# Clustered attention and a gated MLP on one core: key tiles of exp with their own users, no constant matmuls, a new order

## The chip, the cores and the metric

One Trainium2 chip, one core. The metric is the device time of one execution in microseconds (us). The kernel before took 648.9 us, the median of three runs (647.11 to 650.06).

## The reference

Masked attention over 4 batches, 8 heads, 768 positions of 64 values, then an MLP with a spatial gate for each batch. All in fp32.

```
q_assign = argmax(q/|q| @ centroids/|c|, -1); k_assign = argmax(k/|k| @ centroids/|c|, -1)   # 16 clusters
scores = where(q_assign[:, None] == k_assign[None, :], q @ k.T / 8, -1e9)
attn = softmax(scores); x = attn @ v                        # per head; heads side by side: x is 768 x 512
h = relu(x @ w_in); u, v = h[:, :512], h[:, 512:]           # w_in 512 x 1024
v_n = (v - mean(v)) / sqrt(var(v) + 1e-6)
out = (u * (w_spatial @ v_n + b_spatial[:, None])) @ w_out  # w_spatial 768 x 768, w_out 512 x 512
```

## The kernel before

**Numbers in two halves.** Every fp32 factor that needs its precision is split in an fp16 high half and an fp16 low half, and one product is the sum of the products of the halves. So each group of matmuls has a `hi` and a `lo` part.

**The work.** There are 16 head pairs, n = 0 to 15, four of them per batch. A pair goes through `prep` (load, split, cluster logits on PE, argmax on DVE), `shifts` (per head: plain scores on PE at L1029 and their maxima on DVE at L1036, each maximum 128x512; then two 0/1 flag columns and a shift column written by ACT at L1055 and L1058, turned by DMA and put back as extra rows of the factors) and `attend` (L1167). In `attend`, for each head and two key tiles at a time: three score groups of two matmuls (L1204, L1206), three exps on ACT (L1211) that write fp32 into a tile `p32`, for each of the two key tiles a CAST on ACT to the fp16 high half (L1226) and a subtraction on POOL for the low half (L1227), and 18 value matmuls on PE (L1233). The heads of pairs 9, 11, 13 and 15 go through `turned` (L1082) instead, with the queries on the partitions: scores L1104 and L1106, maxima on DVE L1114, a scale column `sl` and a bias column `bi` on DVE (L1127, L1128 per tile; L1130, L1131 two tiles at once in pair 15), exp L1140, cast L1150, POOL L1151, a DMA transpose L1152, and value matmuls L1159 to L1161. After each four pairs `mlp(b)` (L1294) runs the MLP of that batch: 324 matmuls of 512 columns at L1305, in groups of 6: tiles of v, tiles of u, the spatial product, and the output tiles, with ACT, DVE and POOL between them.

**Buffers.** PSUM results come from one ring `r_acc` with 8 banks, each given to whoever is next. The fp32 results of exp come from a ring of two tiles `p32`, each holding a pair of key tiles:

```
r_p32 = R(wk, "p32", [P, 2, S], F32, P32_BUFS)          # P32_BUFS = 2
```

In this ring the tile of two pairs ago must be released by all its users, so by the POOL subtractions of both key tiles, before the first exp of the new pair may be written.

**What sets the order.** The kernel writes no instruction directly. Each `op` names its engine, its cost and what it waits for; the class `Plan` (L310) then runs a small model of the core and puts one operation after another into the program, at each step on the engine that could start first the ready one with the smallest due time. The due times are a table of numbers, `STARTS`, one per operation in the order in which the operations are declared. The model adds two pads: `LATE_PAD` to the end of DMAs of the later stages, and `PE_PAD` to the lag of anything that PE waits for. So an operation is put where the model says that its inputs are there, a little later than it would be without pads. What the chip then does is wait for semaphores in the order written.

**Constant matmuls.** `keep_warm` (L658) declares matmuls of a tile of ones with itself (L662), 512 columns, whose result nobody reads. Their key is so high that the plan takes one only where PE has nothing else ready at that moment. There are 145 of them from the list `WARM` (model times from 2.0 us on) and 5 (`WARM_END`) ahead of the last output tile. All of the 145 write one PSUM token, so one bank of the eight is held from the first of them to the last:

```
tok, o = r_acc.new(), None
...
    o = op("PE", 0.2145, run, after=after, at=at, use=[tok] if k else [], new=[] if k else [tok], cols=512, key=FILLER + k, mms=1)
```

## Time and profile before

| | us |
|---|---|
| median of three runs | 648.9 |
| the runs | 647.11, 650.06, 648.9 |
| profiled execution, its own time | 649.11 |
| span of that execution | 647.3 |
| PE busy | 631.8 (98%) |
| ACT busy | 466.3 (72%) |
| POOL busy | 442.2 (68%) |
| DVE busy | 419.6 (65%) |
| DMA engines, share of the span (queues q1, q10, q8, q14) | 61.0%, 3.0%, 0.6%, 0.1% |
| chain that ended last | PE 68%, ACT 5%, DVE 3%, DMA 2%, issue 1%, POOL 1% |

The time of an execution is its span and 1.8 us around it. Busy time of PE counts the whole run of a matmul; since matmuls overlap in the array, a row that says 0.38 us for one of 512 columns does not mean that the next one starts 0.38 us later. The granted clock (`PEclk`) is a share of full speed.

### The profile page before, as it was taken

The page shows a single profiled execution, that of the slowest core. Times are in us where ns is not written, and L with a number is a line of the kernel's source. Part 1 is how long each engine was busy: PE and PEld are TensorE (multiplying, and loading weights), DVE is VectorE, ACT ScalarE, POOL GpSimd, SP SyncE. Part 2 cuts the span into 40 slices and gives each one's busy share as a digit, 9 for nine tenths or more (in the row PEclk, how much of TensorE's full clock was granted, in tenths as well). Part 3 has the DMA queues.
Part 4 walks back from the last instruction along what each step waited for, and adds up shares of the span by engine and source line. Part 5 has one row for each costly group of instructions (what it writes and reads, how often), then busy time and mean ns, then how long its engine had stood idle before and what let it go on. Part 6 is the DMA issues. An engine that isn't in the chain of part 4 may idle for free.

```text
span 647.3 us, 16908 instructions
## 1 busy us (share of the span) xinstructions
PE 631.8 (98%) x6753; PEld 381.7 (59%) x6753; DVE 419.6 (65%) x845; ACT 466.3 (72%) x879; POOL 442.2 (68%) x376
## 2 busy tenths in 40 slices
PE   8999999999999999999999999999999999999997
PEld 3577767776666765546555755565556555444443
DVE  5989799898999977665776796477523860231000
ACT  5789889899999995536887997689778864232121
POOL 3577888878999995337777885698789964253020
PEclk9999999999999999999999999999999999999999
DMA  6676977697557767622778897976883579212233
GB/s 191 151 126 153 158 172 180 141 174 172 135 123 177 164 139 143 144 60 66 166 157 157 176 217 135 169 156 137 144 155 74 101 142 199 58 34 65 55 76 98
DMA packets 175173, 88.01 MB, mean 136 GB/s; under 512 B 159315, under 2 KB 162422, under 8 KB 175094
## 3 DMA queue, kind: packets, MB, share of 16 engines
q1 hardware_dynamic: 171350, 80.24, 61.0%
q10 hardware_dynamic: 3744, 6.69, 3.0%
q8 instruction: 53, 0.87, 0.6%
q14 instruction: 26, 0.21, 0.1%
HBM read 27.66 MB, written 6.29 MB: 52 GB/s over the span
## 4 chain that ended last, share of the span: by engine, by line
PE 68%; ACT 5%; DVE 3%; DMA 2%; issue 1%; POOL 1%; POOLq 0%; ACTq 0%
PE acc L1305 37%; PE acc L1233 9%; PE acc L1204 5%; PE acc L1206 5%; PE acc L1029 4%; ACT p L1140 2%; PE acc L1104 2%; PE acc L1106 2%; DMA pt<-pt 2%; PE acc L662 1%; DVE nm L1114 1%; PE acc L1159 1%; PE acc L1160 1%; PE acc L1161 1%; DVE lo L912 1%
## 5 line engine op out<-in xcount | busy, mean ns | idle before, releaser
L1227 POOL TENSOR_TENSOR pt<-p,pt 128x768 f16<-128x768 f32 x136 | 226.8, 1687 | 36.2 <-ACT pt L1226 26.8
L1036 DVE TENSOR_REDUCE nm<-acc 128x1 f32<-128x512 f32 (+1 forms) x216 | 137.4, 680 | 25.3 <-PE acc L1029 23.1
L1211 ACT ACTIVATE p<-acc 128x512 f32<-128x512 f32 x216 | 118.7, 607 | 22.4 <-PE acc L1206 12.5
L1305 PE MATMUL acc<-win,xT 128*128 128x512 f16 x576 | 134.1, 379 | 0.1
L1226 ACT CAST pt<-p 128x768 f16<-128x768 f32 x136 | 111.1, 845 | 10.6 <-PE acc L1233 3.5
L1305 PE MATMUL acc<-vn,wsp 128*128 128x512 f16 x432 | 100.7, 379 | 0.0
L1233 PEld LDWEIGHTS <-pt 128*128 128x128 f16 x2448 | 87.8, 97 | 15.8 <-issue 0.7
L1151 POOL TENSOR_TENSOR pt<-p,pt 128x768 f16<-128x768 f32 x48 | 79.3, 1664 | 25.8 <-ACT pt L1150 21.7
L1233 PE MATMUL acc<-vhl,pt 128*128 128x65 f16 x2448 | 93.2, 193 | 0.3 <-POOL pt L1227 0.3
L1305 PEld LDWEIGHTS <-xT 128*128 128x128 f16 x576 | 54.8, 98 | 61.5 <-issue 0.5
L1204 PE MATMUL acc<-hq,lo 128*128 128x512 f16 (+1 forms) x288 | 82.0, 325 | 1.5 <-ACT p L1211 1.3
L1206 PE MATMUL acc<-hq 81*128 81x512 f16 (+1 forms) x288 | 82.2, 326 | 0.3 <-DMA hq<-sht 0.3
L1029 PE MATMUL acc<-hq 80*128 80x512 f16 (+1 forms) x288 | 71.4, 325 | 2.6 <-ACT p L1211 2.4
L1377 POOL TENSOR_TENSOR ghl<-u,ghl 128x512 f16<-128x512 f32 x24 | 27.8, 1157 | 64.8 <-ACT ghl L1376 63.6
L1305 PE MATMUL acc<-wou,gT 128*128 128x512 f16 x288 | 67.7, 379 | 1.1 <-ACT o L1395 0.6
L1305 PEld LDWEIGHTS <-wsp 128*128 128x128 f16 x432 | 40.9, 97 | 46.0 <-issue 0.2
L1140 ACT ACTIVATE p<-acc,bi,sl 128x512 f32<-128x512 f32 (+1 forms) x96 | 57.1, 680 | 12.1 <-POOL pt L1151 7.3
L1375 DVE SCALAR_TENSOR_TENSOR u<-acc,bsp,u 128x512 f32<-128x512 f32 x24 | 17.9, 748 | 69.8 <-PE acc L1305 69.7
L1114 DVE TENSOR_REDUCE nm<-acc 128x1 f32<-128x512 f32 (+1 forms) x72 | 46.3, 682 | 11.1 <-PE acc L1106 11.0
L1305 PEld LDWEIGHTS <-gT 128*128 128x128 f16 x288 | 27.6, 98 | 32.9 <-DMA gT<-ghl 1.1
L662 PE MATMUL acc<-ones 128*128 128x512 f16 x150 | 44.3, 397 | 1.6 <-DVE ones L621 1.6
L1150 ACT CAST pt<-p 128x768 f16<-128x768 f32 x48 | 39.3, 842 | 7.3 <-DMA pt<-pt 5.9
(156 smaller groups left out, 1055.6 us busy)
## 6 DMA issues: line engine op xcount, KB each, us to landing
raw<-in_kqT_dram SPq DMA_DIRECT2D x15, 768.0 KB
vraw<-in_vp_dram SPq DMA_DIRECT2D x16, 384.0 KB
out_dram<-o ACTq DMA_DIRECT2D x24, 256.0 KB
hq<-hq SPq DMA_DIRECT2D x15, 384.0 KB
vn<-in_w_in_dram SPq DMA_DIRECT2D x8, 512.0 KB
hq<-lo SPq DMA_DIRECT2D x15, 192.0 KB
lo<-hq SPq DMA_DIRECT2D x15, 192.0 KB
wraw<-in_wsT_dram SPq DMA_DIRECT2D x12, 192.0 KB
```

Source lines behind the costliest of these rows:

```text
L1029: T.matmul(out=acc.t[:, c:c + cs.stop - cs.start], lhsT=hq.t[0:R_SH, 1, h, t * P:(t + 1) * P], rhs=hq.t[0:R_SH, 0, h, cs], start=c == 0, s ...
L1036: V.tensor_reduce(out=nm.t[:, t, k:k + 1] if n == 1 else nm.t[:, t:t + n, k], in_=src, axis=AX.X, op=ALU.max, negate=True)
L1114: V.tensor_reduce(out=nm.t[:, t, k:k + 1] if n_ == 1 else nm.t[:, t:t + n_, k], in_=src, axis=AX.X, op=ALU.max, negate=True)
L1140: A.activation(out=p32.t[:, j, halves[x]], in_=sc.t[:, j * (S - 512):(j + 1) * (S - 512)] if x else sc.t, func=AF.Exp, bias=bi.t[:, t:t + ...
L1151: c = op("POOL", 1.64, lambda pt=pt, j=j, p32=p32: G_.tensor_tensor(out=pt.t[:, S:], in0=p32.t[:, j, :], in1=pt.t[:, 0:S], op=ALU.subtract ...
L1204: T.matmul(out=o, lhsT=lo.t[:, h, ks], rhs=hq.t[:, 2, h, cs], start=x == 0, stop=False, skip_group_check=True)
L1206: T.matmul(out=o, lhsT=hq.t[0:R_E, 0, h, ks], rhs=hq.t[0:R_E, 1, h, cs], start=False, stop=True, skip_group_check=True)
L1211: o = op("ACT", 0.6, lambda: A.activation(out=p32.t[:, j0:j0 + n_, cs], in_=sc.t.rearrange("p (t c) -> p t c", t=n_), func=AF.Exp, bias=P_ ...
L1226: o = op("DVE" if fast else "ACT", C_CAST if fast else 0.83, lambda pt=pt, p32t=p32t, fast=fast: (V.tensor_copy if fast else A.copy)(out=p ...
L1227: o = op("POOL", 1.64, lambda pt=pt, p32t=p32t: G_.tensor_tensor(out=pt.t[:, S:], in0=p32t(), in1=pt.t[:, 0:S], op=ALU.subtract), after=[o ...
L1233: T.matmul(out=a[:, c * W:c * W + w], lhsT=lhsT, rhs=rhs, skip_group_check=True, **f)
L1305: T.matmul(out=acc.t[:, 0:w], lhsT=lr[m][0], rhs=lr[m][1], start=(m == 0), stop=(m == n - 1))
```

## The change

- `p32` is one constant tile of four key tiles, with two rings of two: in each pair of key tiles each one has a ring of its own, and is released by its own cast, subtraction and value matmuls. The memory is the same as before, 4 x 768 fp32 values on each partition.
- The 150 constant matmuls are gone (`WARM` and `WARM_END` empty), and with them the PSUM bank that they held.
- The two flag columns of a head are written by one ACT instruction (128x6x2) instead of two of 128x6; 25 fewer in all. The low half of the value sums (`wl`) is written in fp16 by DVE directly, which drops 12 ACT instructions at L804. `bsp` is scaled on POOL instead of DVE, once. In pair 15 `sl` and `bi` are computed per tile, as in pairs 9, 11 and 13: 12 + 12 DVE instructions of one column instead of 6 + 6 of two.
- Both pads are zero, and `STARTS` is a new table. The options `FLAG_POOL` and `SHC_POOL` are empty.

The diff, cut (`STARTS` is shown by a part of its first row):

```diff
-MEAN_LOG = 11
...
-LATE_PAD = 0.4
+LATE_PAD = 0.0
+EARLY_PAD = 0.0
...
-PE_PAD = 0.1
+PE_PAD = 0.0
...
 STARTS = (
-    "c-rmR)0Uu3kcHuNWJcuI)vR_`wOMW3wr$(CZQHhO+qP|U{<AroE131(#Ix5H3|L&2pVeSV*d<n*t!2;IDAt<AWARx83ug...
+    "c-jruV}l+#5J2H1lbP^cwcGA)ZQHhO+qP}nwr$(CZQH*0Kb+^oiO%9N#UfY&7RuVNIIK2X%6hR(44GuWh-v1TWrjJ%STK...
...
-WARM = (2.0, 2.3, 2.6, ...
-WARM_END = 5
+WARM = ()
+WARM_END = 0
...
-TS1 = (9, 11, 13)
+FLAG_POOL = ()
+SHC_POOL = ()
...
-            early = not o.tag or o.tag.startswith("p1") or o.tag[0] in "pcvwmf" and o.tag[1] == "0"
-            o.dma, o.post = o.dma * part, o.post + (0.0 if early else LATE_PAD)
+            o.dma, o.post = o.dma * part, o.post + (LATE_PAD if o.tag else EARLY_PAD)
...
-    r_p32 = R(wk, "p32", [P, 2, S], F32, P32_BUFS)
+    p32s = const.tile([P, 4, S], F32, name="p32")
+    r_p32 = [R(None, "p32%d" % j, None, None, 2, tiles=[p32s[:, 2 * (i ^ j) + j] for i in range(2)]) for j in range(2)]
...
-        o = op("DVE", 0.07, lambda: V.tensor_scalar(out=bsp, in0=bsp, ...
+        o = op("POOL", 0.22, lambda: G_.tensor_scalar(out=bsp, in0=bsp, ...
...
-        l_ = op("DVE", 0.3, lambda: V.scalar_tensor_tensor(out=w32.t[:, :, 0:m], in0=svr(), ...
-        l_ = op("ACT", 0.28, lambda: A.activation(out=wl.t[:, :, 0:m], in_=w32.t[:, :, 0:m], func=AF.Copy, scale=2.0 ** MEAN_LOG), ...
+        l_ = op("DVE", 0.28, lambda: V.scalar_tensor_tensor(out=wl.t[:, :, 0:m], in0=svr(), ...
...
-                for c in range(2):
-                    u = 2.0 ** (-MEAN_LOG * c)
-                    cols.append(op("ACT", 0.22, lambda ...: A.activation(out=sx.t[:, t0:t1, R_E + c], ..., bias=-u, scale=2 * u / LIM), ...))
+                def flags(nl=nl, sx=sx, t0=t0, t1=t1):
+                    src = nl.t[:, t0:t1].unsqueeze(2).broadcast_to([P, t1 - t0, 2])
...
+                        A.activation(out=sx.t[:, t0:t1, R_E:R_END], in_=src, func=AF.Relu, bias=-1.0, scale=2.0 / LIM)
+                cols.append(op(*(("POOL", 0.25) if n in FLAG_POOL else ("ACT", 0.23)), flags, after=[o, c_sh, m_half], use=[nl, sx], key=KS))
...
-            p32 = r_p32.new()
+            p32 = [r.new() for r in r_p32]
...
-            if n in TS1:
-                ys = []
-                for t in range(t0, t0 + 2):
...
-            else:
-                o = op("DVE", 0.14, lambda z=z: V.tensor_scalar(out=sl.t[:, z], in0=nl.t[:, z], ...
-                o = op("DVE", 0.15, lambda z=z: V.scalar_tensor_tensor(out=bi.t[:, z], in0=nl.t[:, z], ...
-                ys = [o, o]
+            ys = []
+            for t in range(t0, t0 + 2):
...
-                c = op("ACT", 0.83, lambda ...: A.copy(out=pt.t[:, 0:S], in_=p32.t[:, j, :]), after=got, use=[p32], new=[pt], key=K_HI)
+                c = op("ACT", 0.83, lambda ...: A.copy(out=pt.t[:, 0:S], in_=p32[j].t), after=got, use=p32[j:j + 1], new=[pt], key=K_HI)
```

The change in `attend` is the same in kind as the last lines: each user names `p32[k % 2]` where it named `p32`, and the exp that spans two key tiles writes a slice of `p32s`.

**How the order moves.** On PE at the start, before, around the first maxima of the second head pair: `hq` are the factors, `acc` PSUM banks, `ones` the constant tile.

```order
L662 LDWEIGHTS ones_76
L662 MATMUL acc0_112<-ones_76 128x512
L1029 LDWEIGHTS hq_177
L1029 MATMUL acc2_114<-hq_177 128x256
L1029 LDWEIGHTS hq_177
L1029 MATMUL acc2_114<-hq_177 128x256
L662 LDWEIGHTS ones_76
L662 MATMUL acc0_112<-ones_76 128x512
L1029 LDWEIGHTS hq_177
L1029 MATMUL acc6_118<-hq_177 128x512
```

The same place after the change:

```order
L1026 LDWEIGHTS hq_171
L1026 MATMUL acc6_119<-hq_171 128x512
L1026 LDWEIGHTS hq_171
L1026 MATMUL acc0_113<-hq_171 128x256
L1026 LDWEIGHTS hq_171
L1026 MATMUL acc0_113<-hq_171 128x256
L1026 LDWEIGHTS hq_171
L1026 MATMUL acc4_117<-hq_171 128x512
L925 LDWEIGHTS hq_269
L925 MATMUL acc1_114<-cmw_96,hq_269 128x2x16
```

The constant matmuls between the L1029 matmuls (L1026 after the change) are gone, the bank `acc0` that they wrote holds scores, and the cluster logits of the next pair (L928, now L925) stand right behind.

On PE in the middle of the program, before, where the value matmuls of a key tile (`pt`) end and the first MLP matmuls of a later tile (`win`, `xT`) begin:

```order
L1233 MATMUL acc2_114<-vhl0_84,pt2_107 128x65
L1233 LDWEIGHTS pt2_107
L1233 MATMUL acc2_114<-vhl0_84,pt2_107 128x64
L1233 LDWEIGHTS pt2_107
L1233 MATMUL acc2_114<-vhl0_84,pt2_107 128x65
L662 LDWEIGHTS ones_76
L662 MATMUL acc0_112<-ones_76 128x512
L1305 LDWEIGHTS xT1_100
L1305 MATMUL acc6_118<-win_98,xT1_100 128x512
L1305 LDWEIGHTS xT1_100
```

After the change, in the middle as well, at the end of a spatial group (`wsp`, `vn`):

```order
L1301 LDWEIGHTS wsp_101
L1301 MATMUL acc0_113<-vn_103,wsp_101 128x512
L1301 LDWEIGHTS wsp_101
L1301 MATMUL acc0_113<-vn_103,wsp_101 128x512
L1301 LDWEIGHTS wsp_101
L1301 MATMUL acc0_113<-vn_103,wsp_101 128x512
L1106 LDWEIGHTS hq_3251
L1106 MATMUL acc5_118<-lo_3290,hq_3251 128x512
L1108 LDWEIGHTS hq_3251
L1108 MATMUL acc5_118<-hq_3251 128x512
```

Before, a constant matmul stands between value matmuls and MLP matmuls; after, score matmuls follow the MLP matmuls at once, and `acc0` holds a spatial product.

On ACT, before, where the flag columns (`shx`) are written from the maxima (`nl`) of a head, among the exps of another:

```order
L1211 ACTIVATE p32_776<-acc2_114 128x512
L1055 ACTIVATE shx0_81<-nl_773 128x6
L1058 ACTIVATE shx0_81<-nl_773 128x6 x2
L1211 ACTIVATE p32_776<-acc5_117 128x512
L1211 ACTIVATE p32_776<-acc6_118 128x2x256
L1226 CAST pt1_106<-p32_776 128x768
```

After the change:

```order
L1052 ACTIVATE shx0_81<-nl_491 128x6
L1058 ACTIVATE shx0_81<-nl_491 128x6x2
L1207 ACTIVATE p32_110<-acc2_115 128x512
L1222 CAST pt1_106<-p32_110 128x768
L1207 ACTIVATE p32_110<-acc5_118 128x512
L1207 ACTIVATE p32_110<-acc0_113 128x2x256
```

Two instructions at L1058 became one that writes both columns.

## Rows read from the trace of the kernel before

The window views list, for each stretch, its length and then per engine busy us and instructions in brackets, in the order PE, PEld, DVE, ACT, POOL, then the granted clock, the DMA share and GB/s.

**Rows 1.** Stages of the span: length, then busy us (instructions) per engine.

```profile
0.00:50.00 50.00, 46.91 (x490) 28.34 (x491) 40.22 (x109) 37.31 (x74) 28.02 (x38) 1.00 0.68 156
50.00:147.00 97.00, 93.61 (x1343) 69.33 (x1341) 88.25 (x158) 87.97 (x180) 77.97 (x53) 1.00 0.77 162
147.00:350.00 203.00, 201.55 (x2228) 122.62 (x2226) 158.92 (x291) 161.18 (x312) 157.54 (x135) 1.00 0.63 139
350.00:550.00 200.00, 196.51 (x2252) 119.20 (x2251) 116.99 (x261) 156.32 (x275) 154.37 (x118) 1.00 0.78 151
550.00:647.30 97.30, 93.18 (x447) 42.19 (x445) 15.19 (x29) 23.49 (x41) 24.31 (x35) 1.00 0.27 64
```

**Rows 2.** The same stages, the constant matmuls of line 662 alone.

```profile
0.00:50.00 50.00, 23.05 (x79) 7.95 (x79) 1.00 0.68 156
50.00:147.00 97.00, 10.88 (x37) 3.58 (x37) 1.00 0.77 162
147.00:350.00 203.00, 7.96 (x28) 2.47 (x26) 1.00 0.63 139
350.00:550.00 200.00, 1.14 (x3) 0.30 (x3) 1.00 0.78 151
550.00:647.30 97.30, 1.24 (x5) 0.49 (x5) 1.00 0.27 64
```

**Rows 3.** Timeline of PE in the run's middle: start, duration, line.

```profile
308.52 1.24 PE L662 MATMUL acc<-ones 128*128 128x512 f16 x5
309.60 0.71 PE L1233 MATMUL acc<-vhl,pt 128*128 128x65 f16 x18
```

**Rows 4.** Timeline of PE where its first MLP matmuls stand.

```profile
146.41 0.81 PE L662 MATMUL acc<-ones 128*128 128x512 f16 x3
147.05 2.32 PE L1305 MATMUL acc<-win,xT 128*128 128x512 f16 x10
```

**Rows 5.** Stretch 297 to 310 us, the MLP matmuls of line 1305 alone.

```profile
297.00:310.00 13.00, 1.46 (x6) 0.58 (x6) 1.00 0.24 63
```

**Rows 6.** Waits of DVE: total us, times, longest.

```profile
DVE nm L1036 <- PE acc L1029: 23.1, 25, 4.3
...
DVE nm L1114 <- PE acc L1106: 11.0, 13, 2.3
```

**Rows 7.** Waits of ACT, the same columns.

```profile
ACT p L1140 <- POOL pt L1151: 7.3, 5, 1.8
ACT p L1211 <- POOL pt L1227: 7.2, 5, 2.3
```

**Rows 8.** DVE's groups by line and form: count, busy us, mean ns.

```profile
L1036 DVE TENSOR_REDUCE nm<-acc 128x1 f32<-128x512 f32 x144 | 94.8, 680 | 21.0 <-PE acc L1029 20.2 <-ACT hq L878 0.7
...
L774 DVE SCALAR_TENSOR_TENSOR vhl<-vraw,vhl 128x768 f16<-128x768 f32 x11 | 12.3, 1114 | 6.9 <-ACT vhl L762 6.9
...
L1128 DVE TENSOR_SCALAR bi<-nl,sl 128x1 f32<-128x1 f32 x36 | 5.9, 206 | 0.0
...
L1131 DVE SCALAR_TENSOR_TENSOR bi<-nl,sl 128x2 f32<-128x2 f32 x6 | 4.4, 735 | 0.1
...
L1127 DVE TENSOR_SCALAR sl<-nl 128x1 f32<-128x1 f32 x36 | 3.8, 145 | 0.3
...
L1130 DVE TENSOR_SCALAR sl<-nl 128x2 f32<-128x2 f32 x6 | 3.0, 505 | 0.1
```

**Rows 9.** ACT's groups by line and form.

```profile
L1058 ACT ACTIVATE shx<-nl 128x6 f16<-128x6 f32 x46 | 8.5, 237 | 0.0
...
L804 ACT ACTIVATE wl<-w 2x128 f16<-2x128 f32 x8 | 2.4, 298 | 0.6 <-DVE w L803 0.6
```

**Rows 10.** Timeline of PE at the start.

```profile
1.65 5.67 PE L662 MATMUL acc<-ones 128*128 128x512 f16 x15 [1.65 <-DVE ones L621]
```

**Rows 11.** Timeline of ACT and PE at the end.

```profile
641.02 2.77 PE L1305 MATMUL acc<-wou,gT 128*128 128x512 f16 x12 [0.61 <-ACT o L1395]
...
643.83 0.60 ACT L1395 ACTIVATE o<-acc 128x512 f32<-128x512 f32 x1 [2.80 <-PE acc L1305]
```

More of the change, by code (lines that the diff above doesn't have):

```diff
@@ L43 @@
 R_OH, R_SH, R_E, R_END = 64, 80, 81, 83
-P32_BUFS = 2
 DUE_0 = 56.04
@@ L732, in late_weights @@
         ld = op("ACT", 0.06, lambda: A.dma_start(out=bsp, in_=b_sp), dma="misc", at=40.0)
-        o = op("DVE", 0.07, lambda: V.tensor_scalar(out=bsp, in0=bsp, scalar1=2.0 ** (WS_LOG + VN_LOG), scalar2=None, op0=ALU.mult), after=[ld])
+        o = op("POOL", 0.22, lambda: G_.tensor_scalar(out=bsp, in0=bsp, scalar1=2.0 ** (WS_LOG + VN_LOG), scalar2=None, op0=ALU.mult), after=[ld])
         w_ops["bsp"] = [o]
@@ L1139, in ex @@
                     def ex(sc=sc, x=x, j=j, t=t, p32=p32):
-                        A.activation(out=p32.t[:, j, halves[x]], in_=sc.t[:, j * (S - 512):(j + 1) * (S - 512)] if x else sc.t, func=AF.Exp, bias=bi.t[:, t:t + 1], scale=sl.t[:, t:t + 1])
-                    new = not got and j == 0
-                    e = op("ACT", (0.6, 0.4)[x], ex, after=[ys[j]], use=[sc, sl, bi] + ([] if new else [p32]), new=[p32] if new else [], key=K_EXP)
+                        A.activation(out=p32[j].t[:, halves[x]], in_=sc.t[:, j * (S - 512):(j + 1) * (S - 512)] if x else sc.t, func=AF.Exp, bias=bi.t[:, t:t + 1], scale=sl.t[:, t:t + 1])
+                    e = op("ACT", (0.6, 0.4)[x], ex, after=[ys[j]], use=[sc, sl, bi] + (p32[j:j + 1] if got else []), new=[] if got else p32[j:j + 1], key=K_EXP)
                     exps.append(e)
@@ L1184, in attend @@
                 if k % 2 == 0:
-                    p32 = r_p32.new()
+                    p32 = [r.new() for r in r_p32]
                     done = []
@@ L1210, in unit @@
                     n_ = len(spans)
-                    o = op("ACT", 0.6, lambda: A.activation(out=p32.t[:, j0:j0 + n_, cs], in_=sc.t.rearrange("p (t c) -> p t c", t=n_), func=AF.Exp, bias=P_LOG * LN2, scale=SC_UNIT), after=[o, m_half], use=[sc, p32] if done else [sc], new=[] if done else [p32], key=K_EXP)
+                    o = op("ACT", 0.6, lambda: A.activation(out=p32[j0].t[:, cs] if n_ == 1 else p32s[:, 2 * p32[0].i:2 * p32[0].i + 2, cs], in_=sc.t if n_ == 1 else sc.t.rearrange("p (t c) -> p t c", t=n_), func=AF.Exp, bias=P_LOG * LN2, scale=SC_UNIT), after=[o, m_half], use=[sc] if n_ == 1 else [sc] + p32, new=p32[j0:j0 + 1] if n_ == 1 else [], key=K_EXP)
                     exps.append(o)
@@ L1225, in attend @@
                     fast = (h, k) in CAST_V.get(n, ())
-                    o = op("DVE" if fast else "ACT", C_CAST if fast else 0.83, lambda pt=pt, p32t=p32t, fast=fast: (V.tensor_copy if fast else A.copy)(out=pt.t[:, 0:S], in_=p32t()), after=got, use=[p32], new=[pt], key=K_HI, port=fast)
-                    o = op("POOL", 1.64, lambda pt=pt, p32t=p32t: G_.tensor_tensor(out=pt.t[:, S:], in0=p32t(), in1=pt.t[:, 0:S], op=ALU.subtract), after=[o], use=[p32, pt], key=K_LO)
+                    o = op("DVE" if fast else "ACT", C_CAST if fast else 0.83, lambda pt=pt, p32t=p32t, fast=fast: (V.tensor_copy if fast else A.copy)(out=pt.t[:, 0:S], in_=p32t()), after=got, use=p32[k % 2:k % 2 + 1], new=[pt], key=K_HI, port=fast)
+                    o = op("POOL", 1.64, lambda pt=pt, p32t=p32t: G_.tensor_tensor(out=pt.t[:, S:], in0=p32t(), in1=pt.t[:, 0:S], op=ALU.subtract), after=[o], use=[p32[k % 2], pt], key=K_LO)
                     got = [o]
```

132 lines of the change are left out of this document (64 added, 68 removed).

## The prediction

> **What bounds the kernel now.** I read the windows by stage first [rows 1]. In every stage PE is the fullest engine: busy 46.91 of 50 us, 93.61 of 97, 201.55 of 203, 196.51 of 200, 93.18 of 97.3. DVE comes second only in the first 147 us (40.22 and 88.25 us). So the end is set by PE: the PE work, and what PE does while real work is missing. The same windows with the constant matmuls alone [rows 2] show that part of this busy time is no work: 79 of them in the first 50 us, 37 up to 147 us, 28 up to 350 us, 3 up to 550 us, 5 at the end (a few are counted on both sides of a border; there are 150). The timeline gives their price [rows 3]: five started at 308.52, the next matmul at 309.60, so each held PE for 1.08 / 5 = 0.216 us, and 150 for 32.4 us. That is no gain by itself. A constant matmul stands where the plan had nothing else for PE, and without it PE may just wait.
>
> Whether it does depends on the reserve. The MLP matmuls of a finished batch are work that waits for little, so the plan can fill holes with them. The first starts at 147.05 us, with constant matmuls right ahead of it [rows 4]: up to there no reserve exists. In 297 to 310 us only six MLP matmuls ran [rows 5], and this is where the five at 308.52 us stand: the reserve was used up. After 550 us there is nothing but MLP.
>
> **The change part by part.** The sum is made against the profiled execution, 649.11 us, which is 0.2 above the median of 648.9.
>
> *A. The late constant matmuls.* Behind 147 us there are 28 + 3 = 31 [rows 2]; 31 x 0.216 = 6.7 us. In this stretch the new order has a reserve to put in their place: in the built order 324 MLP matmuls (all of batch 0) stand on PE ahead of the first score of pair 9 before, and 234 after, so 90 x 0.216 = 19.4 us of such work are kept for later, more than 6.7. I take -6.7. The bounds: 0, if PE waits where they stood, and -11.6, if the other idle time behind 147 us goes too. That idle time is 203 - 201.55 + 200 - 196.51 + 97.3 - 93.18 = 9.1 us [rows 1], of which 647.3 - 643.83 = 3.5 us lie behind the last matmul and 0.6 ahead of the last group [rows 11], which leaves 4.9.
>
> *B. The first 147 us.* Here no reserve exists, and the 79 + 37 constant matmuls [rows 2] give nothing back unless what PE waits for comes sooner. What it waits for is the chain of maxima and exps. DVE waits for the scores of a maximum 25 times, 23.1 us in all [rows 6], and ACT's exps wait for POOL's subtractions 5 + 5 times, 7.3 + 7.2 us [rows 7]. Two parts of the change act on these: one more PSUM bank for work (eight instead of seven while constant matmuls ran, so scores can run ahead of the maxima), and key tiles of `p32` that are released one by one. From 50 to 147 us DVE was idle for 97 - 88.25 = 8.75 us [rows 1], and that is the most that this can give. I take half, -4.4, since the first maxima of a pair wait for a DMA or a copy of their factors too. Against it stands that the new order has more work ahead of the first MLP matmul: on DVE five more maxima, 5 x 0.68 = 3.4 us, and one more low half of v, 1.1 us [rows 8], on PE 2.8 us more matmuls by the spacing of 0.216. What DVE does more than PE, 3.4 + 1.1 - 2.8 = 1.7 us, is waiting for PE. So B is -4.4 + 1.7 = -2.7. The bounds: -8.75 and, if neither bank nor rings give anything, +1.7.
>
> The Trainium skill, page "Perfetto Trace Analysis", section Optimization Strategy, says that consistent bubbles can mean that there isn't enough SBUF or PSUM to allocate the next tile. By that sentence the bank would be the cause and B would go to its end of -8.75; rows 6 only show that the waits for scores exist, not that a bank was missing.
>
> *C. ACT's 37 instructions less.* 25 flag writes of 0.237 us and 12 casts of 0.30 us [rows 9] are 5.9 + 3.6 = 9.5 us of ACT over the whole run. In the first 147 us ACT is busy 37.31 + 87.97 us [rows 1]. The casts and flags sit between exps, so a part might shorten the chain. About a third, 3.1 us, lies there (8 flag writes 1.9, 4 casts 1.2). DVE is the fuller engine of that stretch, so I take 0; the bounds are -3.1 and 0. Behind 147 us PE covers it; if PE's cover were gone it would be a gain too.
>
> *D. The clock at the start.* The first 15 constant matmuls took 5.67 us [rows 10], 0.378 each, against 0.216 later: PE began at the lower level, 1.2 GHz, and was at 2.4 GHz before the first real matmul. The granted clock reads 1.00 for every stage [rows 1]. Now the first real matmuls start on the lower level. Of the 46.91 us of PE in the first 50, 23.05 were constant matmuls [rows 1, 2], so 23.9 us are work. If half of it runs at half the clock, it needs 12 us more, against 79 x 0.216 = 17.1 us that the constant matmuls leave free: so nearly all of it fits in the holes, except where a maximum waits for its score. I take +1.0. The bounds are 0 and +6, a quarter of the work at half the clock and none of it in a hole (23.9 / 4).
>
> *E. Pair 15's scale and bias columns.* 6 x (0.505 + 0.735) = 7.4 us become 12 x (0.145 + 0.206) = 4.2 us [rows 8]. DVE is no bound there (116.99 of 200 us, [rows 1]), so of 3.2 us I take -0.5 for a first exp that waits for its column; the bounds are -3.2 and 0.
>
> *F. The end.* The last group of 12 matmuls waits 0.61 us for an ACT instruction [rows 11]; the five constant matmuls ahead of it are on no path. If PE fell to the lower clock in their place, the last 12 would take 12 x 0.216 = 2.6 us longer. I take 0; the bounds are 0 and +2.6. `bsp` on POOL happens once, early, beside POOL's idle time (28.02 busy of the first 50 us): 0.
>
> The sum: -6.7 - 2.7 + 0 + 1.0 - 0.5 + 0 = -8.9, so 640.2 against the profiled execution and **640.0** against the median.
>
> **The rivals.**
>
> *R1, the holes come back.* PE waits where the constant matmuls stood, because what it waits for is late on the chip and not in the plan. For it: after 147 us the holes are next to value matmuls [rows 3], which wait for POOL. Against it: the reserve of 19.4 us. A gives 0, B half, the rest cancels: about 648.
>
> *R2, the clock stays low (slower).* The constant matmuls kept PE busy while it was half empty: 23.9 us of work in 50. Without them PE may go back to the lower clock in the holes of the first stage, and stay there in the next one, where PE has 97 - 93.61 + 10.88 = 14.3 us that are no work [rows 1, 2]. At half the clock, the 82.7 us of work left there would need far more than fits. If the lower clock lasts for another third of it, 27.6 us of work take 27.6 us longer, 14.3 of that in the holes: +13.3. With A's -6.7 that is about 656. Point of decision: a granted clock below 1.00 past about 50 us. Against it: the largest holes of PE in the trace of before, up to 1.3 us, came without a fall of the clock, which reads 1.00 in each stage.
>
> The Trainium skill, page "TensorE: Matmul & The Clock Gate", Part 1, says that the array's default is the throttled clock and that activity releases it. By this rule the removal of the constant matmuls has a price, and R2 is it; the trace of before agrees only as to the start [rows 10].
>
> *R3, an order without pads waits more (slower).* The pads moved PE's work behind its inputs. Without them the plan puts a value group at the moment at which its DMA ends in the model; what is late on the chip is then waited for, with all of PE's queue behind it. 48 turned value groups x 0.4 us of `LATE_PAD` = 19.2 us at most; with half of that on PE, +9.6, less A's 6.7 and with nothing from B: about 652. Against it: the DVE and POOL work beside it.
>
> *R4, a larger gain.* A at -11.6, B at -8.75, C at -3.1, D at 0: 625.
>
> **How the numbers follow.** The forecast, all of A and a part of B, gets 0.57. R1 gets 0.22, R2 0.07, R3 0.07, R4 0.07. Half a per cent, 3.2 us, is what a measurement of this kernel can tell from no change; the bounds are 645.7 and 652.1. Faster: 0.57 + 0.07 + a little of R1, 0.66. Same: most of R1 and a third of R3, 0.20. Slower: R2 and two thirds of R3, 0.14 with what is not named. The range: downward the forecast with B at its end and A as taken (640 - 6.1 = 634) and a part of R4, so 631; upward over R1 and R3, 653. Outside lie most of R2 and half of R4, with what is not named some 15 to 20 in 100. The forecast's own range is 633 to 645.
>
> **What would show it.** In the changed profile: PE's busy time falls by about 32 us and more, its idle time before 147 us rises, and idle time behind 147 us stays under 10 us (A). The first MLP matmul starts at about 147 us or some us earlier (B); it has 2.8 us more PE work ahead of it. DVE's waits for L1029's scores fall below 23.1 us, and the exps' waits for POOL below 14.5 us. The granted clock is below 1.00 at most in the first few slices (D). The forecast is wrong if PE's waits after 147 us grow by as much as the constant matmuls held, if value matmuls wait for DMAs often, or if the clock column shows the lower level beyond 50 us.

## The result: slower by three quarters of a per cent

The changed kernel took 653.53 us, the median of 12 runs (650.95 to 657.22), against 648.95 us of the kernel before (647.11 to 650.06, 12 runs). The ratio is 1.0074, 95% interval 1.0056 to 1.0091. The forecast was 640.0, range 631 to 653. The profiled execution took 651.69 us with a span of 649.9.

PE lost the 150 constant matmuls and did not get the time back. Its busy time fell by 631.8 - 612.5 = 19.3 us and not by the 32 that the forecast named as a sign: in the first 50 us PE is busy for 34.11 us, where 23.9 us before were work, since the matmuls there now take longer (last section). The page of the changed kernel:

```profile
PE 612.5 (94%) x6603; PEld 372.0 (57%) x6603; DVE 414.9 (64%) x856; ACT 462.3 (71%) x842; POOL 443.1 (68%) x377
```

The stages of the changed kernel, columns as in [rows 1]:

```profile
0.00:50.00 50.00, 34.11 (x361) 22.05 (x362) 35.59 (x97) 34.55 (x66) 28.15 (x39) 1.00 0.67 170
50.00:147.00 97.00, 93.15 (x1385) 70.25 (x1383) 93.19 (x177) 90.06 (x174) 82.04 (x53) 1.00 0.74 155
147.00:350.00 203.00, 193.68 (x2241) 119.35 (x2239) 162.68 (x302) 160.87 (x299) 154.50 (x131) 0.99 0.74 151
350.00:550.00 200.00, 198.32 (x2152) 117.68 (x2148) 108.23 (x255) 152.83 (x263) 155.21 (x123) 1.00 0.74 136
550.00:649.90 99.90, 93.22 (x477) 42.65 (x475) 15.19 (x29) 23.95 (x41) 23.18 (x34) 0.99 0.29 67
```

Behind 147 us PE is not busy for 203 - 193.68 + 200 - 198.32 + 99.9 - 93.22 = 17.7 us. Before it was 9.1 us [rows 1], and 31 x 0.216 = 6.7 us of constant matmuls [rows 2, 3]: 15.8 us without work. So 15.8 us became 17.7, where the forecast wanted 9.1. The first MLP matmul starts at 146.47 us (147.05 before [rows 4]), and the waits that the new rings and the bank were to shorten are shorter. ACT's and then DVE's waits in the changed kernel, columns as in [rows 6, 7]:

```profile
ACT p L1207 <- POOL pt L1223: 3.4, 5, 1.1
ACT p L1207 <- POOL pt L1147: 3.1, 3, 1.4
...
ACT p L1137 <- POOL pt L1147: 0.6, 1, 0.6
```

```profile
DVE nm L1033 <- PE acc L1026: 15.4, 11, 5.0
DVE nm L1116 <- PE acc L1108: 15.4, 12, 3.7
```

The exps wait 7.1 us for POOL instead of 14.5, and the maxima of L1033 wait 15.4 us for their scores instead of 23.1. The maxima of the `turned` heads (L1116, before L1114) went the other way, from 11.0 to 15.4 us [rows 6].

Where the time went shows when one counts, up to each moment, the real matmuls that have started, each at the spacing to the next that its form has in the trace of before (0.216 us for 512 columns; some 591 us in all). The table gives how far a kernel is ahead (+) of the kernel before, in us of this work, in its one profiled execution; the experiments are told below.

| at us | 60 | 150 | 180 | 220 | 260 | 360 | 540 |
|---|---|---|---|---|---|---|---|
| changed | -4.0 | +3.5 | +2.8 | -5.6 | -6.4 | -1.6 | -0.9 |
| e1: before, no constants | -1.3 | -1.1 | -1.2 | -0.9 | -0.7 | +0.4 | +1.1 |
| e7: before, constant p32 | -1.0 | +3.7 | +3.7 | +3.6 | +3.3 | +4.5 | +5.5 |
| e12: e7, no constants, less ACT | -1.2 | +4.8 | +4.9 | +4.9 | +4.6 | +5.6 | +7.1 |
| e9: the changed kernel once more | -7.2 | -2.2 | -3.3 | -8.7 | -10.6 | -7.0 | -6.3 |
| e16: e12 planned without pads | -3.0 | +3.0 | +3.2 | +1.5 | -1.9 | -0.7 | -16.7 |

So the changed kernel gained 3.5 us up to 150 us, lost 9.9 up to 260, regained 5.5 up to 540 and lost 1.7 at the end: together the 2.6 us by which the profiled executions differ (651.69 - 649.11). Most of the loss has one place: 8.4 of the 9.9 us fall between 180 and 220 us. The stretch in the changed kernel, and then in e12:

```profile
180.00:225.00 45.00, 38.39 (x508) 25.21 (x506) 35.78 (x59) 37.66 (x74) 36.23 (x29) 0.96 0.78 146
```

```profile
180.00:225.00 45.00, 44.49 (x568) 28.95 (x567) 41.11 (x72) 41.90 (x82) 42.47 (x37) 1.00 0.76 163
```

From 180 to 225 us no engine of the changed kernel is full: PE 38.39 of 45 us, ACT 37.66, DVE 35.78, POOL 36.23. In e12 each of them does 4.2 to 6.2 us more there. That is a stretch of waits on each other. What ended PE's waits from 180 to 230 us, and the granted clock in its middle:

```profile
PE acc L1229 <- ACT p L1207: 2.0, 1, 2.0
PE acc L1200 <- ACT p L1207: 1.8, 3, 0.8
...
PE acc L925 <- ACT p L1207: 0.4, 1, 0.4
```

```profile
208.00:212.00 4.00, 4.00 (x45) 2.75 (x42) 0.88 (x2) 2.41 (x7) 2.99 (x2) 0.57 1.28 156
```

PE is idle for 45 - 38.39 = 6.6 us between 180 and 225 us, and about 4.2 us of that end with an exp on ACT. The four microseconds at a granted clock of 0.57 cost some 4 x 0.43 = 1.7 us more (an estimate from that row). Together they make up about the 8.4 us.

What could have filled these waits stands elsewhere in the new order. The MLP matmuls in the kernel before and then in the changed kernel, alone:

```profile
147.00:260.00 113.00, 42.43 (x180) 17.08 (x179) 1.00 0.67 150
260.00:540.00 280.00, 152.26 (x655) 61.49 (x656) 1.00 0.71 141
```

```profile
147.00:260.00 113.00, 30.60 (x131) 12.29 (x129) 0.98 0.73 148
260.00:540.00 280.00, 162.91 (x705) 66.49 (x704) 1.00 0.73 140
```

From 147 to 260 us the changed kernel runs 49 MLP matmuls fewer, 10.6 us by the spacing of 0.216, and from 260 to 540 us 50 more. From 185.3 to 211.18 us it starts none; e12 starts four groups of six there. Two pieces of the stretch, PE and then ACT:

```profile
203.99 0.38 PE L1200 MATMUL acc<-hq,lo 128*128 128x256 f16 x2 [0.61 <-ACT p L1207]
...
207.65 0.34 PE L1229 MATMUL acc<-mean,hq 83*128 83x65 f16 x6 [2.05 <-ACT p L1207]
...
208.49 0.62 PE L1200 MATMUL acc<-hq,lo 128*128 128x512 f16 x1
...
211.18 1.69 PE L1301 MATMUL acc<-win,xT 128*128 128x512 f16 x6
212.71 0.38 PE L1026 MATMUL acc<-hq 80*128 80x512 f16 x1
```

```profile
204.56 1.52 ACT L1346 ACTIVATE v<-v,y,y 128x512 f32<-128x512 f32 x2
205.98 1.12 ACT L1349 CAST vn<-v 128x512 f16<-128x512 f32 x2
207.01 0.59 ACT L1207 ACTIVATE p<-acc 128x512 f32<-128x512 f32 x1
...
212.81 0.52 ACT L687 ACTIVATE wsp<-wraw 128x384 f16<-128x384 f32 x1 [2.40 <-DMA wraw<-in_wsT_dram]
```

PE waits 2.05 us, to 207.65, for an exp that stands on ACT behind four instructions of the MLP's norm (204.56 and 205.98), and ACT itself waits 2.40 us at 212.81 for a piece of w_spatial that has not landed. Right behind PE's wait the scores at 208.49 take 0.62 us instead of 0.38: the clock fell. That the missing MLP matmuls are what turned ACT's lateness into idle time of PE is argued from these rows; the one run that was to test it did not (e10).

### The profile page after: what moved, and what is told of

It reads as the page before. It is cut to its first block, busy times and chain, and to the rows that moved or that the text cites. A ratio compares the mean times of both kernels' runs of the same rounds, so it can differ in the third digit from the quotient of the medians.

```text
span 649.9 us, 16627 instructions
## 1 busy us (share of the span) xinstructions
PE 612.5 (94%) x6603; PEld 372.0 (57%) x6603; DVE 414.9 (64%) x856; ACT 462.3 (71%) x842; POOL 443.1 (68%) x377
## 4 chain that ended last, share of the span: by engine, by line
PE 52%; DVE 14%; DMA 12%; ACT 11%; issue 6%; POOL 3%; SPq 1%; POOLq 0%; ACTq 0%; DVEq 0%
PE acc L1301 31%; PE acc L1229 7%; DVE nm L1033 5%; DMA wraw<-in_wsT_dram 3%; ACT p L1207 3%; DMA gT<-ghl 3%; PE acc L1200 3%; PE acc L1202 3%; PE acc L1026 3%; ACT pt L1222 2%; ACT p L1137 2%; DMA pt<-pt 2%; DMA hq<-oht 2%; POOL pt L1223 2%; DVE nm L1116 1%
## 5 line engine op out<-in xcount | busy, mean ns | idle before, releaser
L1223 POOL TENSOR_TENSOR pt<-p,pt 128x768 f16<-128x768 f32 x136 | 229.7, 1707 | 40.5 <-ACT pt L1222 25.5
L1033 DVE TENSOR_REDUCE nm<-acc 128x1 f32<-128x512 f32 (+1 forms) x216 | 139.3, 680 | 16.5 <-PE acc L1026 15.4
L1207 ACT ACTIVATE p<-acc 128x512 f32<-128x512 f32 x216 | 122.5, 606 | 21.9 <-PE acc L1202 15.1
L1147 POOL TENSOR_TENSOR pt<-p,pt 128x768 f16<-128x768 f32 x48 | 79.6, 1665 | 30.5 <-ACT pt L1146 23.2
L1229 PEld LDWEIGHTS <-pt 128*128 128x128 f16 x2448 | 89.5, 98 | 16.7 <-POOL pt L1223 1.8
L1229 PE MATMUL acc<-vhl,pt 128*128 128x65 f16 x2448 | 95.6, 193 | 1.4 <-POOL pt L1223 1.1
L1200 PE MATMUL acc<-hq,lo 128*128 128x512 f16 (+1 forms) x288 | 83.5, 331 | 4.2 <-ACT p L1207 2.5
L1202 PE MATMUL acc<-hq 81*128 81x512 f16 (+1 forms) x288 | 83.7, 331 | 0.0
L1026 PE MATMUL acc<-hq 80*128 80x256 f16 (+1 forms) x288 | 74.3, 341 | 5.2 <-DMA hq<-oht 2.4
L1137 ACT ACTIVATE p<-acc,bi,sl 128x512 f32<-128x512 f32 (+1 forms) x96 | 59.0, 683 | 10.5 <-DVE bi L1129 9.8
L1116 DVE TENSOR_REDUCE nm<-acc 128x1 f32<-128x512 f32 (+1 forms) x72 | 46.7, 683 | 15.7 <-PE acc L1108 15.4
L1146 ACT CAST pt<-p 128x768 f16<-128x768 f32 x48 | 40.1, 843 | 13.7 <-DMA pt<-pt 11.3
L1372 ACT CAST ghl<-u 128x512 f16<-128x512 f32 x24 | 14.9, 621 | 40.9 <-DVE u L1371 24.1
```

Source lines behind the costliest of these rows:

```text
L1026: T.matmul(out=acc.t[:, c:c + cs.stop - cs.start], lhsT=hq.t[0:R_SH, 1, h, t * P:(t + 1) * P], rhs=hq.t[0:R_SH, 0, h, cs], start=c == 0, s ...
L1033: V.tensor_reduce(out=nm.t[:, t, k:k + 1] if n == 1 else nm.t[:, t:t + n, k], in_=src, axis=AX.X, op=ALU.max, negate=True)
L1116: V.tensor_reduce(out=nm.t[:, t, k:k + 1] if n_ == 1 else nm.t[:, t:t + n_, k], in_=src, axis=AX.X, op=ALU.max, negate=True)
L1137: A.activation(out=p32[j].t[:, halves[x]], in_=sc.t[:, j * (S - 512):(j + 1) * (S - 512)] if x else sc.t, func=AF.Exp, bias=bi.t[:, t:t + ...
L1147: c = op("POOL", 1.64, lambda pt=pt, j=j, p32=p32: G_.tensor_tensor(out=pt.t[:, S:], in0=p32[j].t, in1=pt.t[:, 0:S], op=ALU.subtract), aft ...
L1200: T.matmul(out=o, lhsT=lo.t[:, h, ks], rhs=hq.t[:, 2, h, cs], start=x == 0, stop=False, skip_group_check=True)
```

## The experiments

The changed kernel scatters: run once more, it came to a ratio of 1.0034 (1.0013 to 1.0054) instead of 1.0074 (e9, told below). Differences of less than some 0.4% between versions of the changed kernel prove nothing. Every ratio is to the kernel before on the same chip.

### The constant matmuls and the clock: e1 to e3

e1, the kernel before with the constant matmuls not issued:

```diff
-                T.matmul(out=tok.t, lhsT=ones, rhs=ones.unsqueeze(1).broadcast_to([P, 4, P]), start=True, stop=True)
+                pass
```

> The kernel before in exactly its own order, with its 150 constant matmuls not issued (the bank that they held stays held). Theory C (the clock: without constant matmuls PE works at the lower clock at the start, and falls back to it for some us after later holes, and that is what the change lost): slower than the kernel before, by 3 to 8 us, about 653, with a granted clock that comes up only near 30 us and falls again at least once. Theory W (waits: the new order lets PE wait between about 185 and 260 us, and the clock costs little): this order has no such waits, so no slower than before, 645 to 649, whatever the clock does.

648.80 us, ratio 0.9983 (0.9964 to 1.0003). The order is the same, and nothing is gained or lost: PE waits where the constant matmuls stood. The clock did come up later:

```profile
0.00:50.00 50.00, 34.79 (x384) 23.73 (x385) 39.06 (x105) 35.77 (x72) 26.64 (x38) 0.93 0.67 151
50.00:147.00 97.00, 90.33 (x1331) 67.77 (x1330) 85.70 (x158) 87.80 (x177) 79.36 (x52) 0.98 0.73 163
```

The granted clock is 0.93 and 0.98 there, and the first of these is too high, since the column does not show the start (last section): at 16.57 us one score of 512 columns takes 0.63 us. The table shows what is lost by it: 1.3 us at 60 us, gone by 360. Theory C falls for this order.

e2 and e3 put constant matmuls into the changed kernel's waits (order otherwise untouched), ahead of the first transpose and, in e3, ahead of 15 more operations:

```diff
+DUMMY = {21: 15}
...
+            for _ in range(DUMMY.get(o.seq, 0)):
+                self.dummy(o.new[0].t)
```

> The changed kernel in exactly its own order, with 15 constant matmuls put ahead of PE's first transpose, into the bank that the transpose writes. PE waits there 7.7 us for DVE, so they fill a wait. Theory C: the clock is up near 7 us instead of 34.1 us; the changed kernel was 4.0 us of PE work behind the kernel before at 60 us, so it gets 2 to 4 us faster, 649.5 to 651.5. Theory W: what was lost at 60 us had been regained by 150 us (3.5 us ahead), and PE waits later anyway: within 1 us of the changed kernel, 653 to 654.

> As the run with the warm start, and 29 more constant matmuls up to 56 us and 28 between 180 and 257 us, each ahead of an operation that PE waited for by 0.4 to 2.7 us, so many as fit in its wait. Same order. Theory C: no fall of the clock at the start or at 208 us: 4 to 6 us faster than the changed kernel, 647.5 to 649.5. Theory W: the waits themselves stay as long, the clock gives back at most 1.7 us for the one fall at 208 us in the profile: 651 to 654.

e2: 652.75 us, 1.0032 (1.0005 to 1.0058). e3: 653.04 us, 1.0060 (1.0035 to 1.0086). Neither gain that theory C named is there beyond the scatter. The first 50 us of e2, and then two stretches of e3:

```profile
0.00:50.00 50.00, 38.92 (x375) 23.63 (x376) 35.43 (x97) 34.54 (x66) 27.99 (x39) 0.76 0.69 169
```

```profile
0.00:50.00 50.00, 40.70 (x388) 23.06 (x388) 33.86 (x95) 34.01 (x64) 27.00 (x39) 0.90 0.69 160
50.00:260.00 210.00, 202.58 (x2785) 141.11 (x2781) 194.66 (x347) 189.05 (x366) 179.64 (x133) 1.00 0.71 153
```

e2 is no test of the clock: its 15 matmuls brought it up, but from 11.3 to 35.2 us it was at the lower level again. e3 is one. Its clock was at full speed from 45 us to the end of the stretch in which the loss lies, and that execution took 651.97 us, as the profile of the result did (651.69); from 180 to 220 us it lost 7.2 us of work all the same. Its two runs with the highest mean granted clock (0.997) took 651.43 and 653.29 us, still more than the 649.27 us of the kernel before on that chip. So the clock is a small part at most of what the changed kernel lost.

### Undoing the plan and the landing tile: e4 to e6

e4, the pads back in the changed kernel (`LATE_PAD` 0.4 with the old rule, `PE_PAD` 0.1), planned with the new table.

> The changed kernel with both pads of the kernel before back (0.4 us at the end of late DMAs, 0.1 us ahead of PE), planned with the new table; no constant matmuls, so the order moves. Theory W, in its form that the missing pads make the waits: 3 to 6 us faster than the changed kernel, 647 to 650, with fewer waits of PE from 185 to 260 us. Theory C: the same start and the same kind of holes, so within 2 us of the changed kernel, 651.5 to 655.

657.08 us, 1.0111 (1.0067 to 1.0155). Both forecasts miss: pads laid onto the new table make it no better.

e5 and e6, the pieces of w_spatial by turns in two halves of the landing tile, in the changed kernel and in the kernel before:

```diff
-... q.dma_start(out=raw.t[:, :n], in_=src), ...
+                z = 384 * (m % 2)
+... q.dma_start(out=raw.t[:, z:z + n], in_=src), ...
```

> The changed kernel in exactly its own order, but the pieces of w_spatial go by turns into the lower and the upper half of their landing tile, so a piece's load no longer waits until DVE has converted the piece before it. Theory P (pieces: in the new order ACT reaches a piece before its load has landed, 4 times and 4.3 us from 150 to 260 us, and exps, casts and PE queue up behind it): the loads are issued earlier, these waits go, and with them most of the 8.4 us of PE work lost between 185 and 225 us; 3 to 6 us faster than the changed kernel, 647.5 to 650.5. Theory R (reserve: the new order keeps 90 MLP matmuls back, so that any lateness becomes idle time of PE): ACT's waits may go, but other lateness takes their place; within 1.5 us of the changed kernel, 652 to 654.

> The same edit on the kernel before, its own order and constant matmuls. There ACT waited for no piece of w_spatial. Theories P and R both: no change, 648 to 650. A gain of over 2 us would mean that the edit does something else than take those waits away.

e5: 655.17 us, 1.0079 (1.0052 to 1.0107). e6: 649.72 us, 1.0001 (0.9985 to 1.0017). e5 tells nothing about theory P, since ACT still waited 3.5 us for pieces from 180 to 230 us.

### The parts of the change in the old order: e7, e8, e11, e12

e7, the kernel before in its own order, constant matmuls and all; only p32 is one constant tile:

```diff
-    r_p32 = R(wk, "p32", [P, 2, S], F32, P32_BUFS)
+    p32s = const.tile([P, 4, S], F32, name="p32")
+    r_p32 = R(None, "p32", None, None, 2, tiles=[p32s[:, 0:2], p32s[:, 2:4]])
```

> The kernel before in exactly its own order, with p32 as one constant tile of four key tiles: the plan still counts a pair as one, but on the chip each key tile is released by its own users. If the new rings are a gain by themselves: the exps' waits for POOL fall from 14.5 us to under 7, and the time by 0 to 2 us, 647 to 649. If they are a part of the loss (more semaphores on ACT, whose event instructions rise as in the changed kernel): 650 or more.

643.83 us, ratio 0.9919 (0.9888 to 0.9949). This is the largest gain of one edit in the study: 5 us faster with not one instruction moved. (The plan still counts a pair as one here; what changed is the tile on which the exps wait.) The exps' waits for POOL, and the first MLP matmul of e7:

```profile
ACT p L1141 <- POOL pt L1152: 3.4, 4, 1.1
...
ACT p L1141 <- POOL pt L1228: 0.2, 1, 0.2
```

```profile
143.30 2.97 PE L1306 MATMUL acc<-win,xT 128*128 128x512 f16 x13
```

3.6 us of waits instead of 14.5, and the reserve begins at 143.30 us instead of 147.05.

e8 adds e1's and e6's edits to e7.

> The kernel before in its own order with no constant matmul issued, the constant p32 tile and the two landing halves. Theory P and R: each part is worth 0 to 2 us in this order, 645.5 to 649; if it lies below 647.5 it beats both kernels. Theory C of the first runs (the clock): slower than the kernel before, 651 or more.

643.31 us, 0.9906 (0.9876 to 0.9936): like e7, so the constant matmuls are worth nothing with the constant tile either.

e11 was to leave ten loads of w_spatial out of e7. Its edit read a variable too late and left nothing out, so it is e7 once more.

> Control for the run with the loads left out: the kernel before with the constant p32 tile (643.8 us in its own run), with the same ten loads left out. Both theories: no ACT wait for pieces stood there, so 642.5 to 645. If the loads cost by filling the DMA queues, this gains as much as the changed kernel does.

643.73 us, 0.9911 (0.9898 to 0.9924): e7 repeats.

e12 is e7 without constant matmuls and with the change's savings on ACT, still in the old order:

```diff
-MEAN_LOG = 11
+MEAN_LOG = 0
...
-... A.activation(out=sx.t[:, t0:t1, R_E + c], in_=nl.t[:, t0:t1], ...)
+... c or A.activation(out=sx.t[:, t0:t1, R_E:R_END], in_=nl.t[:, t0:t1].unsqueeze(2).broadcast_to([P, t1 - t0, 2]), ...)
...
-... V.scalar_tensor_tensor(out=w32.t[:, :, 0:m], ...
+... V.scalar_tensor_tensor(out=wl.t[:, :, 0:m], ...
-... A.activation(out=wl.t[:, :, 0:m], in_=w32.t[:, :, 0:m], ...)
+... None
```

> The kernel before in its own order with the constant p32 tile, no constant matmul issued, both flag columns in one ACT instruction and the low half of the value sums straight from DVE (37 ACT instructions fewer, as in the changed kernel). The forecast's term C says these are worth 0: 642.5 to 645, as with the constant tile alone. If they lie on the path in this order: 640 to 642.5. If the single flag instruction or the unscaled low half costs something: 645.5 or more.

641.29 us, ratio 0.9873 (0.9859 to 0.9888), faster than both kernels. Against e11 on the same chip it is another 2.4 us. So the parts of the change are good by 8 us in the old order. What the changed kernel has besides costs 10.6 us on the same chip (651.87 of e9 against 641.29) and 12.2 by the median of the result: the new table and the pads at zero, and with them what e12 leaves out, which is two rings in the plan instead of one, the freed bank, `bsp` on POOL and pair 15's columns. No run takes these four apart from the table; the last two have no instruction from 180 to 225 us, where most of the loss lies.

### What in the new order costs it: e9, e10, e13 to e15

e9 was to leave out ten loads of w_spatial from the changed kernel; by the same slip as e11 it is the changed kernel once more.

> The changed kernel in exactly its own order; of the twelve pieces of w_spatial only the first two are loaded, and the conversions of the others run on what lies there (the spatial product is left with wrong weights). ACT then waits for no piece. The edit before this one did not take that wait away: ACT still waited 3.5 us from 180 to 230 us, since the loads stood behind other transfers in SP's queue. Theory P (ACT's waits for pieces are the loss): 3 to 6 us faster than the changed kernel, 647.5 to 650.5. Theory R (reserve: MLP matmuls are kept back, and any lateness idles PE): within 1.5 us of the changed kernel, 652 to 654.5, other waits in the place of these.

651.87 us, 1.0034 (1.0013 to 1.0054). As a repeat it shows the scatter, and its profiled execution (657.07 us, span 654.0) shows one source of it. The windows of e9 up to 80 us, and the wait on PE in them:

```profile
0.00:55.00 55.00, 37.51 (x414) 24.48 (x414) 39.38 (x105) 37.66 (x72) 30.07 (x40) 1.00 0.70 163
55.00:67.00 12.00, 9.78 (x81) 7.50 (x82) 6.12 (x12) 4.49 (x10) 3.23 (x2) 0.57 0.33 69
```

```profile
57.22 0.61 PE L1026 MATMUL acc<-hq 80*128 80x512 f16 x1 [2.36 <-DMA hq<-oht]
```

The same wait in the profile of the result:

```profile
55.38 0.39 PE L1026 MATMUL acc<-hq 80*128 80x512 f16 x1 [1.75 <-DMA hq<-oht]
```

PE waited 2.36 us for a DMA, to 57.22, and the granted clock from 55 to 67 us was 0.57. In the profile of the result the wait was 1.75 us long and the clock stayed up. The two executions of the same kernel are 3.2 us apart at 60 us in the table, and 5.7 at 150.

e10, two groups of twelve MLP matmuls ranked earlier:

```diff
+EARLIER = {917: 1345.5, 918: 1350.5, 936: 1355.5, 937: 1360.5}
...
-            o.due, o.key = float(self.starts[len(self.ops)]), 0.0
+            o.due, o.key = float(EARLIER.get(len(self.ops), self.starts[len(self.ops)])), 0.0
```

> The changed kernel with two groups of twelve MLP matmuls (the last v tile and the first u tile of batch 0, 24 x 0.216 = 5.2 us) moved ahead on PE by their due ranks, from 211 to 220 us into the stretch from about 186 to 206 us; what follows is planned again around them. Theory R: PE has them where it waited, and the loss at 185 to 225 us shrinks by 3 to 5 us: 648.5 to 651. Theory P: what waits behind ACT stays late, the groups only change places: 652 to 655.

655.24 us, 1.0095 (1.0069 to 1.0122). Its work fell from +3.3 to -4.8 us between 180 and 220 us, as much as without the edit. But the edit did not do what was meant. Where the MLP matmuls (here L1302) stand on PE in e10:

```profile
209.15 4.00 PE L1302 MATMUL acc<-win,xT 128*128 128x512 f16 x12
...
213.54 2.75 PE L1302 MATMUL acc<-win,xT 128*128 128x512 f16 x12
```

They start at 209.15 instead of 211.18 us. The ranks moved the first dozen ahead of one value group, and from 186 to 206 us, where they were to fill PE's waits, there is still none. So e10 tells nothing about theory R, which stays open.

e13, one copy reads the other half of `lo`, so that the next need not wait for its landing; e14, ten loads of w_spatial really left out; e15, both:

```diff
-        qa1 = sp(lambda: nc.sync.dma_start(out=hq.t[D:P, 2], in_=lo.t[D:P]), ...
+        qa1 = sp(lambda: nc.sync.dma_start(out=hq.t[D:P, 2], in_=lo.t[0:D]), ...
...
-... q.dma_start(out=raw.t[:, :n], in_=src), ...
+... None if skip else q.dma_start(out=raw.t[:, :n], in_=src), ...     # skip=cell == "wsp" and m > 1
```

The waits of SP on which e13 rests, in the changed kernel and in e12:

```profile
SPq L938 <- DMA hq<-lo: 20.1, 7, 5.0
SPq L1081 <- DMA sht<-shx: 19.1, 9, 4.8
```

```profile
SPq L1080 <- DMA sht<-shx: 12.2, 9, 3.7
...
SPq L942 <- DMA hq<-lo: 2.0, 3, 1.2
```

> The changed kernel in exactly its own order; the copy of lo's upper half to hq (hq<-lo) takes lo's lower half instead (the low part of every second head's scores is left wrong), so the copy back into lo's upper half (lo<-hq) no longer has to wait on SP until the first one has landed. In the trace of the changed kernel SP stood 20.1 us in 7 such waits (2.9 us in 4 before), with all later loads behind. Theory Q (queue: without pads SP reaches copies that depend on a landing too early, and everything behind them on SP is late): 2 to 6 us faster than the changed kernel, 648 to 651.5. Theory P (only the pieces of w_spatial, for their own slowness) and theory R (reserve): within 1.5 us, 652 to 655.

> The changed kernel in exactly its own order with ten of the twelve loads of w_spatial really left out (in e9 and e11 a variable was read too late and all twelve were loaded, so those were the changed kernel and e7 once more; the spatial product has wrong weights here). ACT waits for no piece. Theory P: 3 to 6 us faster, 647.5 to 650.5. Theory Q: the pieces are one part of what is late behind SP: 1 to 3 us faster, 650.5 to 652.5. Theory R: 652 to 655.

> Both edits at once, in the changed kernel's own order. Theories P and Q together: 4 to 9 us faster than the changed kernel, 644.5 to 649.5, with the loss of 8 us of PE work from 180 to 225 us gone. Theory R, or a cause not named: 651 or more, the loss still there behind other waits.

e13: 1.0080 (1.0051 to 1.0109), no gain. Its waits of L938 are gone, so theory Q falls for these; SP's waits for DMAs are still 52.6 us in all (62.5 in the changed kernel, 30.3 before), so it does not fall for the others. e14: 652.06 us, 1.0040 (1.0014 to 1.0066). e15: 650.76 us, 1.0032 (1.0013 to 1.0050). ACT's waits for pieces are gone in e14 and e15, and the medians of both lie inside the scatter of the changed kernel. Nor do the profiles show a share for the pieces: from 180 to 220 us the changed kernel loses 8.4 us of work, e14 5.9 and e15 7.8, but e9, the changed kernel once more with all its pieces, loses 5.4. The loss has no single wait that these runs found.

### The pads in the old order: e16 to e18

e12 planned with the pads at zero (e16), with `LATE_PAD` at zero (e17), with `PE_PAD` at zero (e18).

> The kernel of e12 (old table, constant p32 tile, no constant matmuls issued, fewer ACT instructions; 641.3 us) planned with both pads at zero, so the order moves. Theory Q says that the pads kept SP's copies behind their landings: 3 to 8 us slower, 644 to 650, and SP's waits for landings rise from 32 us. If the pads are idle and the new table alone is the loss: 640 to 643.

> The kernel of e12 planned with LATE_PAD at zero and PE_PAD kept at 0.1. Theory S (slack: the pad at the end of late DMAs is what kept PE's and ACT's work behind its transfers): most of the 27.7 us of e16 over e12, 660 to 670. Theory M (match: the table is good only with the numbers it was made with, and any other numbers scramble the order): slower too, but by how much is open, 645 to 670; it is told apart by the next run.

> The kernel of e12 planned with PE_PAD at zero and LATE_PAD kept at 0.4. Theory S: the pad ahead of PE is small, 0 to 5 us slower than e12, 641 to 646. Theory M: a tenth of a us more or less ahead of PE moves as much of the order (as many rows change places as with the other pad), so it loses much too, 650 to 670.

e16: 668.96 us, 1.0307 (1.0293 to 1.0321). e17: 665.02 us, 1.0217 (1.0176 to 1.0258). e18: 658.00 us, 1.0132 (1.0087 to 1.0177). Against e12's 0.9873 these are 28, 22 and 17 us. Taking the tenth of a us ahead of PE away costs most of what the 0.4 us behind DMAs does, and moves as much: PE's order differs from e12's in 2500 of 6603 places in e18, in 2688 in e17. That is theory M's forecast and not theory S's: a table is good with the numbers that it was made with. One stretch of e16, and the same of e12:

```profile
390.00:470.00 80.00, 73.65 (x789) 43.35 (x786) 47.22 (x115) 59.64 (x105) 55.13 (x42) 0.98 0.83 152
```

```profile
390.00:470.00 80.00, 79.37 (x861) 47.65 (x860) 51.16 (x123) 65.68 (x115) 61.17 (x52) 1.00 0.83 159
```

PE is busy 73.65 of 80 us instead of 79.37, and no engine is full: the same picture as in the changed kernel, in another place. Whether slack as such is worth anything stays open: that would need a new table made with the pads (e4 only laid pads onto one made without).

## Why the prediction was wrong

**A, the late constant matmuls (-6.7): the step that failed.** Its sentence was that the new order has a reserve to put in their place, and its bounds ran from 0 to a gain. The reserve was there, but it did its work behind 260 us, with 50 MLP matmuls more and 5.5 us regained. From 147 to 260 us it was kept back, with 49 fewer, and there the changed kernel lost 9.9 us. I read the order only for how many MLP matmuls it keeps, not for when they run and what stands ahead of what on ACT and SP. The sum had no term for an order that loses by itself, and a bound of zero was wrong. e12 shows it: in the old order the parts come to 641.3 us. That this is near the forecast of 640.0 is luck, as it comes by other terms: A is worth nothing there (e1, e8), the constant tile 5 us and ACT's savings 2.4.

**B, the first 147 us (-2.7).** Near in the profile of the result, 3.5 us ahead at 150 us, but partly by luck: in e9 the same kernel is 2.2 us behind there. As a part it holds: e7, with the constant matmuls' bank still held, is 3.7 us ahead at 150 us, against the -4.4 that I gave rings and bank together, and 5 us at the end. So the release of `p32` gives that without the bank; what the bank gives, no run shows. The Trainium skill, page "Perfetto Trace Analysis", section Optimization Strategy, says that consistent bubbles can mean too little SBUF or PSUM for the next tile. In this case 14.5 us of waits became 3.6 with the same bytes of SBUF, by a different release of `p32` alone, and the end of -8.75 that I tied to the PSUM bank has no run behind it.

**C, ACT's savings (0).** Undersized: e12 against e11 is 2.4 us, inside the bound of -3.1. The constant matmuls are gone in e12 too, worth 0.5 us at most by e8 against e7.

**D, the clock at the start (+1.0).** Right for the old order (e1: 1.3 us at 60 us, regained later). In the changed kernel the cost varies: e9 lost 5.7 us more up to 150 us than the profile of the result. Over the 12 runs of the changed kernel time and mean granted clock go together (correlation -0.74): from 651.7 us at 0.996 to 655.2 and 656.1 at 0.979. The mean granted clock is no price, though, as the slow start is counted in some runs and not in others: the profiled execution of e2 has 0.973, with the start in it, and took 652.59 us. In e3, where the start is mostly at full clock, the runs at 0.997 took 651.4 and 653.3 us and those at 0.983 and 0.984 took 654.7 to 657.3. So falls of the clock are a part of the scatter, some 4 us between these runs, and a small part at most of the loss.

**E and F.** E is too small to tell. F missed a wait: 1.7 us of work were lost behind 540 us, where PE waits 3.2 us in two waits for the transposes of `gT`.

**The rivals.** R1's mechanism is what e1 shows: without the constant matmuls the holes come back, for 0. R3 had the sign and the price (about 652), and it had them by luck: PE did not wait for turned value groups but for exps from 180 to 225 us, behind the MLP's norms on ACT, and the pads put back did not help (e4). R2's place was wrong too: the clock did not stay low past 50 us in the profile of the result, it fell once more at 208 us, for about 1.7 us of work. Both slower rivals together had 0.14, and the measured time lies 0.5 us above the range.

**What is shown and what is not.** Shown: the changed kernel's order, with the little that e12 leaves out, costs 10.6 to 12.2 us against the parts in the old order; most of it lies from 180 to 225 us, where no engine is full and PE waits mostly for exps; the constant matmuls are worth nothing in the old order; the loss is there at full clock as well (e3). Not shown: what makes the exps late there, since taking out the waits for pieces (e14) or for `lo` (e13) did not help, and whether MLP matmuls put into that stretch would, since e10 did not put them there.
